# Float64 weights to float32: ScalarE's absolute value and two bounds in one VectorE operation

## The chip, the cores and the metric

The kernel runs on one core of a Trainium2 chip. The metric is the device time of one execution in microseconds (us). A core has five engines, each with an instruction stream of its own that it works through in order: TensorE (PE in the profile, its weight loads PEld), VectorE (DVE), ScalarE (ACT), GpSimd (POOL) and SyncE (SP, which here only issues DMAs).

## The reference, cut to what matters

```python
# attention part: x (8, 8, 512, 64), state (8, 8, 32, 64), float32
a  = softmax(x @ state.T / 8);  xread = a @ state
a2 = softmax(state @ x.T / 8);  sread = a2 @ x
x  = concatenate([xread, sread], axis=2) -> (4608 tokens, 512)
# first feed-forward part; w_gate, w_val (512, 1536), w_out (1536, 512): float64
g = x @ w_gate
x = (g * sigmoid(g) * (x @ w_val)) @ w_out
# second part: 8 experts of 576 tokens each, assigned greedily by the largest logits
logits = x @ gate;  out[mask] = relu(x[mask] @ w1[e]) @ w2[e]
```

The inputs are drawn as float32, but a division by a square root in numpy makes the three weights `w_gate`, `w_val` and `w_out` float64. They come to the chip as pairs of 32-bit words, and the kernel has to make float32 of them itself.

## The kernel before, in words

A matrix product in float32 is made of three: each operand is split into a rounded `hi` (ScalarE, a cast) and the rest `lo` (VectorE or GpSimd, a subtraction), and TensorE adds hi*hi, lo*hi and hi*lo.

There are three phases. The first, up to about 530 us of the profile, makes the hidden rows `ht` of the first feed-forward part; the second makes its output and the routing; the third runs the eight experts. All that follows is in the first phase, and there in its first three of four pairs of batches.

The work of the first phase is cut into 48 items: a pair of batches p (0 to 3) by a slice f of 128 hidden columns (0 to 11). In an item, `prepare` (L238) multiplies the states with the slice's weights (TensorE to `ps_x`), copies the result to `shi` (ScalarE, L258) and subtracts (VectorE, `slo`, L262); `hidden_part` (L264) then makes, for each of the two batches, 12 TensorE products of 512 columns into `pp` (L273), a Silu (ScalarE, `sg`, L277) and a product (VectorE, `ht`, L279). An item ends with its second `ht`, so there are 72 `ht` in the first 36 items.

Beside the items run: the attention of the 8 batches in 16 units (`attention`, L163: scores on TensorE, transposes and reductions on VectorE, two exponentials on ScalarE at L185 and L186, two products on GpSimd), and `narrow` (L69), which makes float32 of a half slice of 128 x 512 float64 numbers. It runs 36 times: 24 times for the gate and value weights, two for each slice f, and 12 times for the output weights (`weights_out`, L344). Slice f is needed by the item of pair 0 and slice f; until then the item waits.

Before the change `narrow` is a chain over the engines: DMA of 512 KB into `raw8`; VectorE bounds the high words (L81), shifts them (L84) and puts sign and exponent together (L85); ScalarE squares the bounded number (L88) and scales the low words (L89); GpSimd adds the two (L91); VectorE sets to zero what is too small (L93); ScalarE makes `hi` (L97) and GpSimd `lo` (L99).

The order on each engine is not written by hand in this part. The program is recorded as a loop over items with generators beside them (`beside`, L433): each `yield n` puts a generator off by n slots, five slots to an item, and the list `starts` (L419) says at which slot a narrowing begins. A scheduler with a timeline simulation then orders each engine's instructions. Only for the last pair of batches (items from `place[DIRECT, 0]` = 36) is TensorE's order fixed as recorded (`manual_schedule`). Silu and the exponentials belong to different ScalarE tables, and between them stands an `ACT_TABLE_LOAD`.

Of the kernel before, what the change touches and what calls it, by code (L numbers as in the profile page):

```python
# [9 lines left out]
F32 = mybir.dt.float32  # L10
F32R = mybir.dt.float32r
BF16 = mybir.dt.bfloat16
I32 = mybir.dt.int32
F16 = mybir.dt.float16
U8 = mybir.dt.uint8
U32 = mybir.dt.uint32
AF = mybir.ActivationFunctionType
OP = mybir.AluOpType
# [17 lines left out]
for _n, _w in (("before", 128), ("iota", 128), ("one", NT), ("rowhi", NT),  # L36
# [2 lines left out]
    CONSTS.append((_n, _o, _o + _w))  # L39
BEHIND = {"start": 36, "first": 26, "count": 19, "sum": 4, "totals": 17, "before": 14, "last": 18, "slots": 46,  # L40
          "places": 24}
LEAST = float(np.array([897 << 20], np.uint32).view(np.float32)[0])
LARGEST = float(np.array([(1150 << 20) | 0xFFFFF], np.uint32).view(np.float32)[0])


# [10 lines left out]
class Program:  # L56
# [12 lines left out]
    def narrow(self, src, hi=None, lo=None):  # L69

        nc, cv = self.nc, self.cv
        raw = cv.tile([128, 512, 2], I32, name="raw8", bufs=2)
        nc.sync.dma_start(raw.rearrange("p c t -> p (c t)"), src)
        yield 3
        c = cv.tile([128, 512], F32, name="cvc", bufs=3)  # L80
        nc.vector.tensor_scalar(c, raw[:, :, 1].bitcast(F32), -LARGEST, LARGEST, op0=OP.max, op1=OP.min)  # L81
        ci = c.bitcast(I32)
        t = cv.tile([128, 512], I32, name="cvt")
        nc.vector.tensor_scalar(t, ci, 3, 0x3FFFFFF8, op0=OP.logical_shift_left, op1=OP.bitwise_and)  # L84
        nc.vector.scalar_tensor_tensor(t, ci, -0x40000000, t, op0=OP.bitwise_and, op1=OP.bitwise_or)  # L85
        yield 1
        sq = cv.tile([128, 512], F32, name="cvs")
        nc.scalar.activation(sq, c, AF.Square)  # L88
        nc.scalar.activation(ci, raw[:, :, 0].bitcast(U32), AF.Copy, scale=2.0 ** -29)  # L89
        yield 1  # L90
        nc.gpsimd.tensor_tensor(t, t, ci, OP.add)  # L91
        yield 1
        nc.vector.scalar_tensor_tensor(c, sq, LEAST * LEAST, t.bitcast(F32), op0=OP.is_ge, op1=OP.mult)  # L93
        if hi is None:
            return c
        yield 1
        nc.scalar.copy(hi, c)  # L97
        yield 1
        nc.gpsimd.tensor_tensor(lo, c, hi.bitcast(F32), OP.subtract)  # L99
# [10 lines left out]

    def states(self, p):

        raw = self.cv.tile([128, 512], F32, name="cvs").rearrange("p (k c) -> p k c", k=4)
        self.nc.sync.dma_start(raw, self.a["sz"][p])
        yield 4
        self.state[p] = [self.sp.tile([128, 4, 128], F32R, name=n) for n in ("sh", "sl")]
        self.split(*self.state[p], raw, self.nc.gpsimd)
# [226 lines left out]
    def weights_out(self, f):  # L344

        nc = self.nc
        wo = yield from self.narrow(self.a["wo"][f // 2][:, 512 * (f % 2):512 * (f % 2) + 512].bitcast(I32))
        nc.sync.dma_start(self.wod[f // 2][:, f % 2], wo)
        yield 2
        pt = self.psl.tile([128, 4, 128], F32, name="ps_m")  # L350
        for k in range(4):
            nc.tensor.transpose(pt[:, k, :], wo[:, 128 * k:128 * k + 128], self.ident)
        yield 2
        both = self.cv.tile([128, 512], F32, name="cvs").rearrange("p (k c) -> p k c", k=4)
        nc.scalar.copy(both, pt)
        yield 2
        if f % 4 == 0:
            self.pf = self.psl.tile([128, 4, 128], F32, name="ps_l")
        for k in range(4):
            nc.tensor.matmul(self.pf[32 * k:32 * k + 32, f % 4, :], self.wg2[:, k, :], both[:, k, :],  # L360
                             start=True, stop=True)
        if f % 4 < 3:
            return
        yield 2
        fs = self.hp.tile([128, 512], F32, name="sg", bufs=2).rearrange("p (f c) -> p f c", f=4)
        nc.scalar.copy(fs, self.pf)
        yield 2
        pt = self.psl.tile([128, 4, 4, 32], F32, name="ps_m")
        for g in range(4):
            nc.tensor.transpose(pt[:, g].rearrange("p k e -> p (k e)"), fs[:, g, :], self.ident)  # L370
        yield 2
        nc.vector.tensor_reduce(self.wl[:, f - 3:f + 1, 0:E], pt[:, :, :, 0:E].rearrange("p g k e -> p g e k"),
                                AX.X, OP.add)

    def phase1(self, pools, first):

        tc, nc, a = self.tc, self.nc, self.a
        self.xp = first.enter_context(tc.tile_pool(name="xp", bufs=4))
        self.hp = first.enter_context(tc.tile_pool(name="hp", bufs=4))
        cv, lg, at, sp = ExitStack(), ExitStack(), ExitStack(), ExitStack()  # L380
# [17 lines left out]
        place = {item: n for n, item in enumerate(order)}  # L398
# [3 lines left out]
        def narrowed(f, m):  # L402
            if m == 0:
                w.append(self.wring.tile([128, 2, 1024], F32R, name="w"))
            q = slice(512 * m, 512 * m + 512)
            yield from self.narrow(a["wgv"][f][:, q].bitcast(I32), w[f][:, 0, q], w[f][:, 1, q])
            done[f] = m
# [10 lines left out]

        starts = []  # L419
        for f in range(1, NF):  # L420
            t = 5 * (place[0, f] - 1) - 8
            gap = 5 if f > LAG else 2
            starts += [(max(t - gap, 0), f, 0), (max(t, 0), f, 1)]

# [8 lines left out]
        def beside():  # L433

            f, rest = divmod(self.slot - self.OUTS, 5)
            if f == rest == 0:
                self.fold_start()
            if 0 <= f < NF and rest == 0:
                self.going.append([self.weights_out(f), 0, self.slot])
            while starts and starts[0][0] <= self.slot:  # L440
                self.going.append([narrowed(*starts.pop(0)[1:]), 0, self.slot])
            self.weights()
            for i, g in enumerate(list(self.going)):
                held = lambda lo, hi: sum(lo <= x[1] <= hi for x in self.going[1:] if x is not g)
                if g[2] > self.slot:
                    continue
                if i and (g[1] == 0 and held(1, 2) > 1 or g[1] == 1 and (held(2, 4) > 1 or held(2, 9) > 2)):
                    continue
                g[1] += 1
                d = next(g[0], None)  # L450
                if d is not None:
                    g[2] = self.slot + d
                elif i:
                    self.going.remove(g)
                else:
                    g[2] = 10000
            self.slot += 1

        def item(n, late):
# [11 lines left out]
            while n and not ready():  # L471
                beside()
            if ready():
                prep = self.prepare(*nxt, w[nxt[1]])
            next(prep, None)
            some(late, 1)
            beside()
            while self.atts.get(2 * p) != 1:
                beside()
# [43 lines left out]
        with tc.manual_schedule(engines={mybir.EngineType.PE}):  # L523
            for n in range(G, len(order)):
                p, f = order[n]
# [688 lines left out]
```

## Time and profile before

| | us |
|---|---|
| median of 3 runs | 1265.61 (1262.04 to 1266.66) |
| the profiled execution's own time | 1275.44 |
| its span, first to last instruction | 1273.5 |
| TensorE busy in the span | 1199.5 (94%) |
| VectorE busy | 822.3 (65%) |
| ScalarE busy | 543.7 (43%) |
| GpSimd busy | 284.0 (22%) |

The profiled execution took 0.8% longer than the median of the runs. The shares are averages over phases with different limits. In the page's slices of 31.8 us, VectorE is at 7 to 9 tenths in the first eight and TensorE at 5 to 8 tenths in the first five; from the sixth on TensorE is at 9.

### The profile page before, as it was taken

What the parts mean: (1) busy time and instruction counts of PE and PEld (TensorE: products, weight loads), DVE (VectorE), ACT (ScalarE), POOL (GpSimd) and SP (SyncE); (2) the same over time, 40 slices, a digit from 0 to 9 for tenths busy, and PEclk for the clock granted to TensorE, in tenths of its full rate; (3) what the DMA queues carried; (4) which work ended last, traced back from release to release, by engine and by line L of the source; (5) the groups of instructions that cost most, each with busy time, mean ns of one, the idle gap of its engine ahead of it and who ended that gap; (6) DMA issues with size and microseconds to landing.
All of it is one profiled execution on the core that took longest, in us unless ns stands there. A gap on an engine that the chain in (4) does not pass through costs nothing.

```text
span 1273.5 us, 21378 instructions
## 1 busy us (share of the span) xinstructions
PE 1199.5 (94%) x8127; PEld 980.6 (77%) x8127; DVE 822.3 (65%) x1730; ACT 543.7 (43%) x935; POOL 284.0 (22%) x247
## 2 busy tenths in 40 slices
PE   5888889999999999999999999979998999999998
PEld 2556668777786667877777777759897999999987
DVE  7999898768664443489989989735653444544310
ACT  4788877777753433411212122123432233343211
POOL 5665451313200000000000000032515135033031
PEclk9889999999999999999999999988998999999999
DMA  7555566345247877532333323257967365443110
GB/s 271 170 170 162 165 192 185 108 126 177 92 140 198 225 216 237 165 130 100 129 104 122 112 100 124 84 156 224 278 219 234 118 199 168 140 137 114 36 36 36
DMA packets 156309, 194.18 MB, mean 152 GB/s; under 512 B 14032, under 2 KB 119504, under 8 KB 156208
## 3 DMA queue, kind: packets, MB, share of 16 engines
q1 hardware_dynamic: 149904, 174.99, 43.9%
q0 software_dynamic: 6304, 17.83, 4.4%
q8 instruction: 64, 1.05, 0.3%
q14 instruction: 37, 0.30, 0.1%
HBM read 137.18 MB, written 55.51 MB: 151 GB/s over the span
## 4 chain that ended last, share of the span: by engine, by line
PE 69%; DVE 12%; issue 8%; ACT 6%; DMA 3%; POOL 1%; another core or an unknown queue 1%; ACTq 0%; SPq 0%; POOLq 0%; DVEq 0%
PE pp L898 18%; PE pp L273 17%; PE pu L1028 13%; PE pd L1063 7%; PE pd L1084 5%; PE ps_x L251 4%; ACT shi L258 2%; PE ps_s L312 1%; DVE cvt L85 1%; DVE slo L262 1%; PE ps_s L663 1%; DVE hlo L876 1%; DVE cvc L81 1%; DVE cvc L93 1%; ACT L277 1%
## 5 line engine op out<-in xcount | busy, mean ns | idle before, releaser
L898 PE MATMUL pp<-w,hhi 128*128 128x512 f32 x816 | 261.8, 398 | 0.0
L1028 PE MATMUL pu<-thi,w 128*128 128x256 f32 (+1 forms) x1024 | 213.6, 295 | 5.1 <-ACT thi L66 2.2
L898 PEld LDWEIGHTS pp<-w,hhi 128*128 128x128 f32 x816 | 151.5, 188 | 33.8 <-issue 2.5
L1028 PEld LDWEIGHTS pu<-thi,w 128*128 128x128 f32 x1024 | 171.5, 195 | 7.4 <-DVE ulo L1031 2.6
L273 PE MATMUL pp<-ahi,shi 128*128 128x512 f32 x384 | 159.3, 416 | 15.1 <-ACT sg L277 7.8
L898 PE MATMUL pp<-w,hlo 128*128 128x512 f32 x408 | 162.3, 398 | 1.2 <-DVE hlo L876 1.2
L262 DVE TENSOR_TENSOR slo<-ps_x,shi 64x512 fp32r<-64x512 f32 x192 | 131.9, 687 | 42.0 <-ACT shi L258 38.8
L273 PE MATMUL pp<-alo,shi 128*128 128x512 f32 x384 | 152.8, 399 | 0.0
L1028 PE MATMUL pu<-tlo,w 128*128 128x288 f32 (+1 forms) x512 | 150.9, 295 | 1.0 <-issue 0.8
L886 ACT CAST hhi<-hlo 128x768 fp32r<-128x768 f32 x68 | 53.4, 833 | 222.1 <-PE pp L898 219.4
L258 ACT CAST shi<-ps_x 64x512 fp32r<-64x512 f32 x192 | 111.5, 581 | 49.0 <-PE ps_x L251 41.8
L1031 DVE SCALAR_TENSOR_TENSOR ulo<-pu,uhi 128x256 fp32r<-128x256 f32 (+1 forms) x128 | 54.7, 437 | 114.2 <-ACT uhi L1030 106.5
L279 DVE TENSOR_TENSOR ht<-pp,sg 128x512 f32<-128x512 f32 (+1 forms) x108 | 71.3, 661 | 79.4 <-PE pp L273 41.3
L273 PE MATMUL pp<-ahi,slo 128*128 128x512 f32 x384 | 117.7, 394 | 0.1
L1030 ACT ACTIVATE uhi<-pu 128x256 fp32r<-128x256 f32 (+1 forms) x128 | 50.2, 398 | 151.1 <-PE pu L1028 128.0
L1063 PE MATMUL pd<-uhi,w 128*128 128x288 f32 x512 | 108.9, 297 | 6.1 <-issue 4.4
L273 PEld LDWEIGHTS pp<-ahi,shi 128*128 128x128 f32 x384 | 73.1, 191 | 46.5 <-ACT sg L277 12.1
L67 DVE TENSOR_TENSOR w<-raw,w 128x1024 fp32r<-128x1024 f32 x56 | 68.4, 1223 | 57.0 <-issue 34.2
L1028 PEld LDWEIGHTS pu<-tlo,w 128*128 128x128 f32 x512 | 99.7, 195 | 0.7 <-issue 0.4
L277 ACT ACTIVATE sg<-pp 128x512 f32<-128x512 f32 (+1 forms) x108 | 61.9, 575 | 79.6 <-PE pp L273 78.2
L1045 POOL DMA_INDIRECT out<-sw,idx x63 | 67.8, 1077 | 111.1 <-DVE sw L1069 93.3
L898 PEld LDWEIGHTS pp<-w,hlo 128*128 128x128 f32 x408 | 76.8, 188 | 18.1 <-DVE hlo L876 1.7
(242 smaller groups left out, 2178.8 us busy)
## 6 DMA issues: line engine op xcount, KB each, us to landing
raw<-w SPq DMA_DIRECT2D x64, 512.0 KB
hlo<-hd SPq DMA_DIRECT2D x34, 768.0 KB
hd<-ht SPq DMA_DIRECT2D x96, 256.0 KB
hraw<-hd SPq DMA_DIRECT2D x144, 128.0 KB
raw<-wgv SPq DMA_DIRECT2D x24, 512.0 KB
yd<-ys SPq DMA_DIRECT2D x32, 256.0 KB
xg<-row SPq DMA_DIRECT2D x28, 256.0 KB
row<-xg SPq DMA_DIRECT2D x112, 64.0 KB
```

What stands on the lines that cost most here:

```text
L67: lo_engine.tensor_tensor(lo, src, hi.bitcast(F32), OP.subtract)
L258: nc.scalar.copy(hi[r[z], b], banks[z][q])
L262: nc.vector.tensor_tensor(lo[r[z], b], banks[z][q], hi[r[z], b].bitcast(F32), OP.subtract)
L273: nc.tensor.matmul(pp, w(ws, k, m), xx[:, k, :], start=i == 0, stop=i == 3 * kt - 1)
L277: nc.scalar.activation(sg, pg, AF.Silu)
L279: nc.vector.tensor_tensor(ht, pv, sg, OP.mult)
L898: nc.tensor.matmul(py, x[:, f, :], wo[f // 2][:, f % 2, ws, :], start=i == 0, stop=i == 3 * NF - 1)
L1028: nc.tensor.matmul(pu, wf[:, ws, k, cs], x[xs][:, k, q], start=i == 0, stop=i == 11)
L1031: nc.vector.scalar_tensor_tensor(lo[:, f, q], pu, 0.0, hi[:, f, q].bitcast(F32), op0=OP.max, op1=OP.subtract)
L1045: st = self.nc.gpsimd.indirect_dma_start(out=out, in_=rows, in_offset=None, out_offset=bass.IndirectOffsetOnAxis(ap=at, axis=0))
L1063: nc.tensor.matmul(pd, wf[:, ws, f % 2, 128 * fb:128 * fb + 128], xs[:, f, T:], start=i == 0, stop=i == 23)
L1084: nc.tensor.matmul(pd, xs[:, f, 128 * t:128 * t + 128], wf[:, ws, f % 2, :], start=i == 0, stop=i == 23)
```

## The change

The magnitude is taken first, on ScalarE (`Abs`, read from the high words in place of VectorE's bounding). One VectorE operation then bounds it from below and above (`LEAST` becomes the least magnitude kept, instead of a threshold below which zero is written), two more shift and join it with the sign, which is read from the raw words. The Square on ScalarE and the last VectorE operation (L93) are gone, and the sum of GpSimd is the result. Buffers: three `raw8` instead of two, one `cvt` and one `cvs` instead of two. Slots: six instead of three between the DMA and the first operation, starts three slots earlier, and up to three narrowings waiting for their DMA instead of two.

```diff
-LEAST = float(np.array([897 << 20], np.uint32).view(np.float32)[0])
+LEAST = float(np.array([896 << 20], np.uint32).view(np.float32)[0])
...
-        raw = cv.tile([128, 512, 2], I32, name="raw8", bufs=2)
+        raw = cv.tile([128, 512, 2], I32, name="raw8", bufs=3)
         nc.sync.dma_start(raw.rearrange("p c t -> p (c t)"), src)
-        yield 3
+        yield 6
         c = cv.tile([128, 512], F32, name="cvc", bufs=3)
-        nc.vector.tensor_scalar(c, raw[:, :, 1].bitcast(F32), -LARGEST, LARGEST, op0=OP.max, op1=OP.min)
         ci = c.bitcast(I32)
-        t = cv.tile([128, 512], I32, name="cvt")
-        nc.vector.tensor_scalar(t, ci, 3, 0x3FFFFFF8, op0=OP.logical_shift_left, op1=OP.bitwise_and)
-        nc.vector.scalar_tensor_tensor(t, ci, -0x40000000, t, op0=OP.bitwise_and, op1=OP.bitwise_or)
+        nc.scalar.activation(c, raw[:, :, 1].bitcast(F32), AF.Abs)
         yield 1
-        sq = cv.tile([128, 512], F32, name="cvs")
-        nc.scalar.activation(sq, c, AF.Square)
-        nc.scalar.activation(ci, raw[:, :, 0].bitcast(U32), AF.Copy, scale=2.0 ** -29)
-        yield 1
-        nc.gpsimd.tensor_tensor(t, t, ci, OP.add)
-        yield 1
-        nc.vector.scalar_tensor_tensor(c, sq, LEAST * LEAST, t.bitcast(F32), op0=OP.is_ge, op1=OP.mult)
+        nc.vector.tensor_scalar(c, c, LEAST, LARGEST, op0=OP.max, op1=OP.min)
+        nc.vector.tensor_scalar(ci, ci, 3, 0x3FFFFFF8, op0=OP.logical_shift_left, op1=OP.bitwise_and)
+        nc.vector.scalar_tensor_tensor(ci, raw[:, :, 1], -0x40000000, ci, op0=OP.bitwise_and, op1=OP.bitwise_or)
+        t = cv.tile([128, 512], I32, name="cvt", bufs=1)
+        nc.scalar.activation(t, raw[:, :, 0].bitcast(U32), AF.Copy, scale=2.0 ** -29)
+        yield 2
+        nc.gpsimd.tensor_tensor(ci, ci, t, OP.add)
...
-            t = 5 * (place[0, f] - 1) - 8
+            t = 5 * (place[0, f] - 1) - 11
...
-                if i and (g[1] == 0 and held(1, 2) > 1 or g[1] == 1 and (held(2, 4) > 1 or held(2, 9) > 2)):
+                if i and (g[1] == 0 and held(1, 2) > 2 or g[1] == 1 and (held(2, 4) > 1 or held(2, 9) > 2)):
```

VectorE, near the start, the second half slice of the first weights (its transfer is `raw_126`), between operations of the first attention units (`sT`, `mx`, `m`). Line numbers after the change are lower by two from the middle of `narrow` on. Before:

```order
L81 TENSOR_SCALAR cvc<-raw_126 128x512
L176 STREAM_TRANSPOSE w<-ps_m 128x512
L181 TENSOR_REDUCE mx<-ps_m 128x1
L84 TENSOR_SCALAR cvt<-cvc 128x512
L188 TENSOR_SCALAR mx<-mx 128x1
L178 TENSOR_REDUCE m_148<-w 128x16
L182 TENSOR_SCALAR mx<-mx 128x1
L190 TENSOR_REDUCE m_141<-sT 128x16
L85 SCALAR_TENSOR_TENSOR cvt<-cvc,cvt 128x512
L189 RECIPROCAL mx<-mx 128x1
L93 SCALAR_TENSOR_TENSOR cvc<-cvs,cvt 128x512
```

And after, the same half slice:

```order
L85 TENSOR_SCALAR cvc<-cvc 128x512
L176 TENSOR_REDUCE m_148<-w 128x16
L188 TENSOR_REDUCE m_141<-sT 128x16
L180 TENSOR_SCALAR mx<-mx 128x1
L187 RECIPROCAL mx<-mx 128x1
L86 TENSOR_SCALAR cvc<-cvc 128x512
L189 TENSOR_SCALAR m_141<-m_141 128x16
L87 SCALAR_TENSOR_TENSOR cvc<-raw_126,cvc 128x512
```

Three operations stand where there were three and then, for the first half slice, L93; no operation of VectorE stands behind GpSimd's sum any more, and the first of the three now reads what ScalarE wrote.

ScalarE, in item 20 of 48, the same attention unit (`es`, `sT`) with its table loads. Before:

```order
L185 ACT_TABLE_LOAD
L185 ACTIVATE es,mx<-ps_s,mx 128x512
L186 ACTIVATE sT<-sT 128x512
L258 CAST shi<-ps_x 64x512 x2
L277 ACT_TABLE_LOAD
L277 ACTIVATE sg<-pp 128x512
```

After:

```order
L183 ACT_TABLE_LOAD
L183 ACTIVATE es,mx<-ps_s,mx 128x512
L275 ACT_TABLE_LOAD
L275 ACTIVATE sg<-pp 128x512
L184 ACT_TABLE_LOAD
L184 ACTIVATE sT<-sT 128x512
L353 COPY cvs<-ps_m 128x512
L83 ACTIVATE cvc<-raw_2654 128x512
L275 ACT_TABLE_LOAD
L275 ACTIVATE sg<-pp 128x512
```

A Silu has moved between the two exponentials of the unit, which makes four loads of two. In the whole program there are 28 loads before and 32 after; behind the 37th `sg` there are 12 and 16.

SyncE, the queue of the DMAs at the start. Before:

```order
L114 DMA cvs<-sz 128x512
L341 DMA wg_2257<-wg 128x4x8
L124 DMA xt<-xt 128x1024
L122 DMA st<-st 128x256
L78 DMA raw_299<-wgv 128x1024
```

After:

```order
L112 DMA cvs<-sz 128x512
L79 DMA raw_295<-wgv 128x1024
L339 DMA wg_2145<-wg 128x4x8
L122 DMA xt<-xt 128x1024
L120 DMA st<-st 128x256
```

The third transfer of weights stands ahead of the inputs of the second batch instead of behind them.

## Rows read from the trace of the kernel before

**Rows 1.** Windows up to 1st, 9th, 25th, 37th, 73rd `ht`: length, busy, clock, DMA.
```profile
core 0: us, PE busy (x) PEld busy (x) DVE busy (x) ACT busy (x) POOL busy (x), PEclk, DMA share, GB/s
0.00:44.80 44.80, 28.79 (x213) 15.71 (x214) 35.33 (x64) 26.30 (x55) 27.40 (x27) 0.85 0.71 240
44.80:110.30 65.50, 50.35 (x381) 34.98 (x380) 62.18 (x112) 56.01 (x100) 42.07 (x32) 0.95 0.53 169
110.30:183.50 73.20, 67.20 (x383) 50.29 (x382) 69.16 (x111) 58.39 (x101) 37.79 (x28) 1.00 0.58 170
183.50:227.50 44.00, 42.48 (x238) 34.09 (x238) 38.11 (x62) 29.94 (x53) 9.04 (x7) 1.00 0.59 185
227.50:383.00 155.50, 152.07 (x987) 118.93 (x986) 107.95 (x187) 110.84 (x192) 33.01 (x26) 1.00 0.42 128
```
**Rows 2.** Instruction groups of VectorE up to 383 us: busy us, mean ns | idle before.
```profile
L93 DVE SCALAR_TENSOR_TENSOR cvc<-cvs,cvt 128x512 f32<-128x512 f32 x36 | 33.1, 919 | 2.4 <-POOL cvt L91 2.2
L85 DVE SCALAR_TENSOR_TENSOR cvt<-cvc,cvt 128x512 int32<-128x512 int32 x36 | 30.6, 851 | 0.2
L81 DVE TENSOR_SCALAR cvc<-raw 128x512 f32<-128x512 f32 x36 | 22.0, 612 | 10.3 <-DMA raw<-wgv 8.7 <-PE ps_x L251 0.7 <-DMA raw<-wo 0.7
L84 DVE TENSOR_SCALAR cvt<-cvc 128x512 int32<-128x512 int32 x36 | 21.4, 594 | 0.4
L178 DVE TENSOR_REDUCE m<-sT 128x16 f32<-128x512 f32 x12 | 8.1, 673 | 0.0
```
**Rows 3.** Instruction groups of ScalarE up to 383 us.
```profile
L89 ACT ACTIVATE cvc<-raw 128x512 int32<-128x512 uint32 x36 | 24.3, 674 | 6.5 <-DVE cvt L85 4.7 <-issue 1.2 <-DVE mx L189 0.2
L88 ACT ACTIVATE cvs<-cvc 128x512 f32<-128x512 f32 x36 | 22.7, 630 | 15.6 <-DVE cvc L81 10.6 <-DVE cvc L93 4.0 <-POOL sl L67 0.8
L277 ACT ACT_TABLE_LOAD x14 | 18.0, 1283 | 0.2
```
**Rows 4.** Instructions of the tile `cvc`: duration ns min/median/max, first and last start.
```profile
L81 DVE TENSOR_SCALAR cvc<-raw x36: 384/427/1527, 7.5 to 312.8; 128x512 f32<-128x512 f32 x36
...
L84 DVE TENSOR_SCALAR cvt<-cvc x36: 362/427/1291, 7.9 to 313.8; 128x512 int32<-128x512 int32 x36
L85 DVE SCALAR_TENSOR_TENSOR cvt<-cvc,cvt x36: 628/683/1728, 9.5 to 315.4; 128x512 int32<-128x512 int32 x36
...
L93 DVE SCALAR_TENSOR_TENSOR cvc<-cvs,cvt x36: 626/688/1781, 15.9 to 331.3; 128x512 f32<-128x512 f32 x36
```
**Rows 5.** ScalarE's waits, 44.8 to 110.3 us: us in total, times, longest.
```profile
ACT cvs L88 <- DVE cvc L81: 2.2, 3, 1.7
...
ACT w L97 <- DVE cvc L93: 1.5, 2, 0.9
```
**Rows 6.** Timeline of ScalarE, 316 to 320 us: start, duration, instruction.
```profile
317.97 1.28 ACT L277 ACT_TABLE_LOAD   x1
319.27 0.60 ACT L277 ACTIVATE sg<-pp 128x512 f32<-128x512 f32 x1
```
**Rows 7.** Timeline of TensorE, same stretch and on, with idle time before.
```profile
319.92 0.50 PE L273 MATMUL pp<-ahi,shi 128*128 128x512 f32 x1 [0.35 <-ACT sg L277]
...
323.77 0.50 PE L273 MATMUL pp<-ahi,shi 128*128 128x512 f32 x1 [1.47 <-ACT sg L277]
```
**Rows 8.** VectorE waiting for a ScalarE cast, up to 420 us.
```profile
DVE slo L262 <- ACT shi L258: 23.8, 22, 3.2
```

More of the change, by code (lines that the diff above doesn't have):

```diff
@@ L111, in states @@
     def states(self, p):
-        raw = self.cv.tile([128, 512], F32, name="cvs").rearrange("p (k c) -> p k c", k=4)
+        raw = self.cv.tile([128, 512], F32, name="cvs", bufs=1).rearrange("p (k c) -> p k c", k=4)
         self.nc.sync.dma_start(raw, self.a["sz"][p])
@@ L353, in weights_out @@
         yield 2
-        both = self.cv.tile([128, 512], F32, name="cvs").rearrange("p (k c) -> p k c", k=4)
+        both = self.cv.tile([128, 512], F32, name="cvs", bufs=1).rearrange("p (k c) -> p k c", k=4)
         nc.scalar.copy(both, pt)
```

## The prediction

> **What bounds the kernel now.** I read the busy shares by slice first, then cut the first 383 us at the starts of the 1st, 9th, 25th, 37th and 73rd `ht`, because two `ht` make an item and the edited code works only there; last the groups of VectorE and ScalarE, and who waits for whom. The reader is to see in [rows 1] five stages, which I call A to E. In A (44.8 us), B (65.5) and C (73.2) VectorE is busy 35.3, 62.2 and 69.2 us. A begins with 7.5 us in which its first instruction (L81, first start in [rows 4]) waits for the weights, so nearly all the rest of these three stages is VectorE at work; TensorE is idle 16.0, 15.2 and 6.0 us. In D (44.0 us) and E (155.5) it turns round: TensorE is idle 1.5 and 3.4 us, VectorE 5.9 and 47.6. What the change saves on VectorE can therefore be cashed up to the 25th `ht` and hardly behind it. ScalarE is no bound now, but near it: 56.0 of 65.5 us in B.
>
> **The change part by part.**
>
> *The removed VectorE operation.* L93 runs 36 times at a mean of 919 ns, 33.1 us [rows 2]. Its median is 688 and its longest 1781 ns [rows 4]: part of the mean is stalls. If the stalls pass to its neighbours, 36 x 0.688 = 24.8 us go; if they go with it, 33.1. I use the mean and keep 24.8 as the other end.
>
> The trace shows the same spread for L85, 628 to 1728 ns [rows 4]. By the Trainium skill ("SBUF — State Buffer", "SBUF: two separate sides") VectorE operations with two SBUF inputs or in a two-port mode and GpSimd operations shut each other out for a whole instruction. By that rule, as GpSimd's work is not cut, the blocked time may move rather than vanish, and the saving over all 36 would be 24.8 instead of 33.1 us.
>
> *The three that stay.* The bounding is now read from a contiguous buffer, the joining (L87) from every second word of the raw data. L81 (every second word) and L84 (contiguous) have the same median of 427 ns [rows 4], so the stride costs nothing measurable there. I keep 612, 594 and 851 ns for the three; the new join is bounded by 0.68 (median of L85) and 0.92 us (mean of L93), which would be 2 us over the 28 by the 25th `ht`, either way.
>
> *ScalarE.* Square (630 ns) becomes Abs, read with a stride like L89 (674 ns) [rows 3]; I take 674, which is +0.04 each, 1.6 us over 36.
>
> *Moves.* Counted in the orders. By the 1st `ht` the four operations of a narrowing had been issued 6, 5, 5 and 4 times; after the change the three stand there 6 times each, and three large attention operations (0.673 us by L178) have moved behind. By the 9th: 15, 14, 14, 13 against 16, 15, 14, and two more attention operations have moved. By the 25th: 25, 25, 24, 24 against 28, 28, 28, and the attention is level again. So the new order runs up to four narrowings ahead.
>
> Stage A: VectorE -4 x 0.919 + 0.594 + 0.851 - 3 x 0.673 = -4.2 us. On SyncE the third transfer of weights now goes ahead of the second batch's inputs: 512 KB at the 240 GB/s of this stage [rows 1] is 2.2 us for those inputs, which I cost at nothing, since the first batch's attention covers it; without that cover it takes half of the gain. Behind GpSimd's sum there is one step less on the way to the first weights, which can make it better. I take -4.2 (between -7 and -2).
>
> Stage B: VectorE -9 x 0.919 + 0.612 - 0.851 - 2 x 0.673 = -9.8 us, to 52.4. ScalarE: two loads fewer (-2.6), 10 Abs for 9 Squares (+1.1), one more Copy (+0.7): -0.8, to 55.2 us. So ScalarE becomes the longer of the two. It was idle 9.5 us of B; of that it waited 2.2 us for L81 and 1.5 us for L93 [rows 5], both of which are gone. I take -0.8 - 3.7 = -4.5 us; the ends are -0.8 (ScalarE keeps all its waits) and -9.8 (it hinders nobody).
>
> Stage C: VectorE -11 x 0.919 + 2 x 0.612 + 2 x 0.594 + 4 x 0.851 + 5 x 0.673 = -0.9 us: what goes is filled with the narrowings run ahead and the attention coming back. ScalarE gets two more narrowings' first step (+1.8) and four more Copies (+2.7), to 62.9 of 73.2 us. I take 0, between -2 and +4.5.
>
> Stage D: VectorE loses over ten us more, but TensorE ends it. It can give back at most its own idle time, -1.5 us [rows 1].
>
> Stage E: four more table loads (16 for 12) of 1.283 us. In the trace a load between the exponentials and a Silu reaches TensorE: the Silu of [rows 6] starts as the load ends, and TensorE stands 0.35 and then 1.47 us in front of the unit whose exponentials were split [rows 7]. By the whole stage, 3.4 us idle for 12 loads is 0.29 each: +1.1 us for four. The ends are 0 and 2 split units at 1.82, +3.6. L93 is gone here too, but VectorE has 47.6 us to spare.
>
> A load takes 1.283 us, with 0.2 us of idle time before all 14 of L277 [rows 3], and the Silu starts 0.02 us behind one [rows 6]. The Trainium skill ("ScalarE: Activation LUTs", "What ACT_TABLE_LOAD costs") adds a drain of about 1.38 us to each: by that, as an estimate, four more would take ScalarE 10.6 instead of 5.1 us. This trace shows no such drain behind a load.
>
> *Sum.* -4.2 - 4.5 + 0 - 1.5 + 1.1 = -9.1 us on the profiled execution's 1275.4: 1266.3. The median of the runs stands at 1265.61 / 1275.44 = 0.9923 of it, so 1256.6 us. Nothing behind 383 us is changed but a few neighbours that trade places, so what is gained stays.
>
> **The rivals.**
>
> 1. *ScalarE hinders nobody* and the stages follow VectorE's sum: -4.2 - 9.8 - 0.9 - 1.5 = -16.4 us, 1249 us. For it: in B VectorE waits for almost nothing now (3.3 us idle). Against it: ScalarE's 55.2 us would have to fit into 55.7.
>
> 2. *ScalarE becomes the bound*: it keeps its waits in B (-0.8), D gives nothing, E has two more split units at 1.82 us: -4.2 - 0.8 + 3.6 = -1.4 us, 1264 us. For it: 86% busy in B and 80% in C already, and the chain now begins on it. Against it: a good part of its waits was for the removed operations.
>
> 3. *VectorE queues behind Abs*, slower. VectorE's first operation waited for a DMA before, which had long landed but for 8.7 us in all [rows 2]; now it waits for a place in ScalarE's order, and behind it stand `slo`, `ht` and the attention, which TensorE needs. Where VectorE waited for a cast of ScalarE, it was 23.8 us for 22 times, 1.08 each [rows 8]. By the 25th `ht` VectorE's sum is 14.9 us lower with 28 such first operations, so the case decides from 0.53 us per Abs on. If three of four wait 1.08, that is 22.7 - 14.9 + 1.1 = +8.9 us, 1274 us. Against it: only a small part of the `slo` waited at all, and the new order puts Abs well ahead of its VectorE operations.
>
> That the change does nothing in the program is excluded by the order: L93 is not in it.
>
> **How the numbers follow.** The forecast has a chance of 0.48, its own range 1251 to 1261; rival 1 0.17 (1244 to 1251), rival 2 0.23 (1259 to 1268), rival 3 0.12 (1266 to 1280). A change under 0.5% (6.3 us) can't be told from none, so faster means under 1259.3. From the forecast 0.43 and all of rival 1, and 0.02 of rival 2: 0.62. Slower than 1271.9 is most of rival 3: 0.09. The rest, 0.29, is the same. The range leaves out the far half of rival 3 and the far end of rival 1: 1244 to 1268.
>
> **What would show it.** Right: the 1st `ht` near 41 us, the 9th near 102, the 25th near 175, the 37th near 217, the 73rd near 374; VectorE's join and bounding at 0.6 to 0.9 us; ScalarE over 90% busy in B. Rival 1 has the 9th `ht` near 96; rival 2 the 9th near 105 and the 73rd near 382; rival 3 a line of VectorE's bounding waiting for ScalarE's Abs with over 15 us. The forecast would be wrong if E loses more than 4 us (table loads in front of TensorE), if the second batch's scores start late because of the moved transfer, or if Abs takes much longer than 0.67 us.

## The result, and the profile after

The changed kernel takes 1252.23 us (median of 4 runs, 1250.44 to 1255.98) against 1265.51 us of the kernel before (4 runs). The ratio is 0.9915 with a 95% interval of 0.9893 to 0.9938, faster by 0.85%. Two later runs on other chips gave 0.9906 (0.9887 to 0.9925) and 0.9911 (0.9891 to 0.9931).

The windows of the changed kernel, cut at the same `ht` as before (1st, 9th, 25th, 37th, 73rd), answer to [rows 1]:

```profile
0.00:39.30 39.30, 23.58 (x204) 12.82 (x208) 30.42 (x58) 26.55 (x53) 26.75 (x26) 0.96 0.81 279
39.30:95.70 56.40, 46.98 (x352) 33.20 (x340) 53.99 (x97) 49.58 (x90) 40.49 (x33) 0.91 0.64 197
95.70:171.10 75.40, 69.34 (x401) 52.10 (x399) 69.16 (x117) 67.61 (x118) 42.36 (x32) 1.00 0.68 204
171.10:217.20 46.10, 45.28 (x245) 33.88 (x246) 26.35 (x39) 24.84 (x45) 2.33 (x2) 1.00 0.32 95
217.20:375.50 158.30, 155.08 (x1016) 120.15 (x1012) 109.77 (x188) 117.31 (x198) 33.07 (x27) 1.00 0.44 130
```

By stage the change is -5.5, -9.1, +2.2, +2.1 and +2.8 us: 12.4 us won up to the 25th `ht`, 4.9 given back up to the 73rd, 7.5 kept. The spans of the two first profiles differ by far more, 22.3 us; the experiments show that most of the rest does not belong to the change.

VectorE's groups up to 380 us answer to [rows 2]. L93 has no successor; L85 is the bounding, L86 the shift, L87 the join:

```profile
L87 DVE SCALAR_TENSOR_TENSOR cvc<-raw,cvc 128x512 int32<-128x512 int32 x36 | 32.8, 911 | 0.3
L86 DVE TENSOR_SCALAR cvc<-cvc 128x512 int32<-128x512 int32 x36 | 24.3, 675 | 0.2
L85 DVE TENSOR_SCALAR cvc<-cvc 128x512 f32<-128x512 f32 x36 | 21.7, 605 | 2.8 <-ACT cvc L83 2.7
```

The four groups of before took 107.1 us, the three take 78.8: 28.3 us less, between the two ends named (24.8 and 33.1). The shift has grown from 594 to 675 ns and the join from 851 to 911: a part of the stalls of L93 went on to its neighbours. In the tile's durations (minimum, median, maximum) shortest and longest lie as in [rows 4], so the operations are not slower by themselves; what holds them is shown at the price of L93 below:

```profile
L85 DVE TENSOR_SCALAR cvc<-cvc x36: 357/428/1492, 9.5 to 303.6; 128x512 f32<-128x512 f32 x36
L86 DVE TENSOR_SCALAR cvc<-cvc x36: 357/476/1401, 10.5 to 304.3; 128x512 int32<-128x512 int32 x36
L87 DVE SCALAR_TENSOR_TENSOR cvc<-raw,cvc x36: 649/692/1662, 11.0 to 305.7; 128x512 int32<-128x512 int32 x36
```

ScalarE's groups, as in [rows 3]; L83 is the Abs:

```profile
L89 ACT ACTIVATE cvt<-raw 128x512 int32<-128x512 uint32 x36 | 24.4, 678 | 2.9 <-POOL cvc L91 2.8
L83 ACT ACTIVATE cvc<-raw 128x512 f32<-128x512 f32 x36 | 24.2, 672 | 11.2 <-DMA raw<-wgv 9.3 <-DMA wod<-cvc 1.5 <-POOL w L97 0.2
L275 ACT ACT_TABLE_LOAD x16 | 20.5, 1283 | 0.3
```

Abs took 672 ns, as estimated from the strided Copy (674). The wait for the weights' DMA, 8.7 us on VectorE before, is now on ScalarE with 9.3 us. What VectorE still waits for up to the 25th `ht` is little:

```profile
DVE sT L174 <- PE ps_s L169: 8.3, 1, 8.3
DVE m L188 <- ACT sT L184: 3.7, 1, 3.7
DVE mx L186 <- ACT es L183: 1.5, 1, 1.5
DVE ht L277 <- ACT sg L275: 1.1, 2, 0.7
DVE w L202 <- POOL w L191: 0.3, 1, 0.3
DVE cvc L85 <- ACT cvc L83: 0.2, 1, 0.2
```

The first line is the start; behind ScalarE VectorE stands 6.5 us in all, and behind Abs 0.2.

### The profile page after: what moved, and what is told of

It is laid out like the page before. It is cut to its first block, busy times and chain, and to the rows that moved or that the text cites. A ratio compares the mean times of both kernels' runs of the same rounds, so it can differ in the third digit from the quotient of the medians.

```text
span 1251.2 us, 21394 instructions
## 1 busy us (share of the span) xinstructions
PE 1191.4 (95%) x8127; PEld 973.5 (78%) x8127; DVE 799.0 (64%) x1694; ACT 548.8 (44%) x939; POOL 278.8 (22%) x247
## 4 chain that ended last, share of the span: by engine, by line
PE 68%; ACT 8%; DVE 8%; DMA 7%; issue 6%; SPq 1%; POOL 1%; POOLq 0%; ACTq 0%; DVEq 0%
PE pp L896 18%; PE pp L271 17%; PE pu L1026 12%; PE pd L1061 6%; PE pd L1082 5%; PE ps_x L249 4%; DMA raw<-w 3%; ACT shi L256 2%; PE ps_s L310 1%; ACT L275 1%; PE ps_s L661 1%; DVE hlo L874 1%; ACT sg L275 1%; SPq L1003 1%; DMA row<-yd,idx 1%
## 5 line engine op out<-in xcount | busy, mean ns | idle before, releaser
L1026 PE MATMUL pu<-thi,w 128*128 128x256 f32 (+1 forms) x1024 | 208.7, 290 | 0.4 <-ACT thi L66 0.4
L271 PE MATMUL pp<-ahi,shi 128*128 128x512 f32 x384 | 158.6, 414 | 13.8 <-ACT sg L275 6.7
L1026 PEld LDWEIGHTS pu<-thi,w 128*128 128x128 f32 x1024 | 168.1, 191 | 0.8 <-ACT thi L66 0.5
L271 PE MATMUL pp<-ahi,slo 128*128 128x512 f32 x384 | 120.5, 398 | 1.0 <-DVE slo L260 1.0
L1043 POOL DMA_INDIRECT out<-sw,idx x63 | 66.9, 1061 | 110.9 <-DVE sw L1067 93.1
```

The lines of the kernel that those rows point to most:

```text
L271: nc.tensor.matmul(pp, w(ws, k, m), xx[:, k, :], start=i == 0, stop=i == 3 * kt - 1)
L1026: nc.tensor.matmul(pu, wf[:, ws, k, cs], x[xs][:, k, q], start=i == 0, stop=i == 11)
L1043: st = self.nc.gpsimd.indirect_dma_start(out=out, in_=rows, in_offset=None, out_offset=bass.IndirectOffsetOnAxis(ap=at, axis=0))
```

## The experiments

All twelve in one table, then one by one. Up to the 25th `ht`, "busy" is VectorE's busy time and "idle" the rest. The times of different chips are not to be compared (chips differ by 6 us here for the same kernel), the ratios are. The 25th `ht` of one kernel depends less on the chip: 183.5 to 186.0 us in three traces of the kernel before, 170.1 to 171.3 in three of the changed one. e1 to e4 ran on one chip, e5 to e8 on a second, e9 to e12 on a third.

| run | median us | ratio to before (95%) | 25th `ht` | VectorE busy | idle | 73rd `ht` |
|---|---|---|---|---|---|---|
| before, first trace | 1265.51 | | 183.5 | 166.7 | 16.8 | 383.0 |
| after, first trace | 1252.23 | 0.9915 (0.9893 to 0.9938) | 171.1 | 153.6 | 17.5 | 375.5 |
| e1 before again | 1270.88 | 1.0008 (0.9987 to 1.0030) | 186.0 | 169.4 | 16.6 | 385.5 |
| e2 new arithmetic, old pace | 1269.04 | 1.0008 (0.9983 to 1.0034) | 180.7 | 154.2 | 26.5 | 383.0 |
| e3 old arithmetic, new pace | 1273.78 | 1.0040 (1.0024 to 1.0056) | 188.6 | 158.5 | 30.1 | 389.9 |
| e4 a fourth operation | 1280.08 | 1.0091 (1.0057 to 1.0124) | 188.2 | 173.9 | 14.3 | 392.4 |
| e5 after again | 1251.19 | 0.9906 (0.9887 to 0.9925) | 171.3 | 154.5 | 16.8 | 375.8 |
| e6 two raw buffers | 1253.69 | 0.9930 (0.9913 to 0.9946) | 177.7 | 152.2 | 25.5 | 376.4 |
| e7 short slots | 1259.89 | 0.9980 (0.9968 to 0.9992) | 176.6 | 159.0 | 17.6 | 380.5 |
| e8 exponentials together | 1258.95 | 0.9976 (0.9961 to 0.9991) | 179.1 | 160.5 | 18.6 | 381.9 |
| e9 before, same chip as e10 | 1262.84 | 1.0005 (0.9991 to 1.0019) | 186.0 | 168.9 | 17.1 | 385.5 |
| e10 after, same chip as e9 | 1250.97 | 0.9911 (0.9891 to 0.9931) | 170.1 | 152.7 | 17.4 | 374.5 |
| e11 no Abs | 1255.26 | 0.9943 (0.9923 to 0.9962) | 180.0 | 162.2 | 17.8 | 378.7 |
| e12 one slot more | 1254.78 | 0.9942 (0.9924 to 0.9960) | 172.8 | 155.7 | 17.1 | 376.2 |

**e1, e9 and e10: which part of the gain is the change's.** Unchanged kernels. Expected of e1, e9 and e10:

> The kernel before, unchanged, once more. Theory: in the first trace of before, 14.5 of the 22.3 us by which its span exceeds that of the changed kernel lie in the expert phase (intervals of 52.4, 55.6 and 50.3 us between experts where 48 is usual), which the change does not touch, so they are that execution's own. Then here the span is near 1263, the 73rd ht again near 383 us and the experts' phase shorter by about 8 us. Rival: the expert phase of before is always that long because of the order of its last instructions; then the phase takes about 416 us from the first pu to the end again, and ratio 1.000 with the earlier runs of before only if all are so.

> The kernel before once more, with the changed kernel behind it on the same chip, for the expert phase (first pu to the end): 413 and 417 us in two traces of before, 402 and 403 in two of the changed kernel, but no two of them from one chip. Theory C (the chip sets it): both phases within 3 us of each other, and the whole gain of 11 to 13 us less than 4 from outside the first 383 us. Theory K (the kernel sets it): before's at least 8 us longer here too.

> The changed kernel on the same chip as the run before it. 73rd ht at 375 to 377 us by either theory; expert phase within 3 us of that of before (theory C) or 8 us shorter (theory K). Ratio 0.989 to 0.993.

The stretch from the first `pu` of the experts to the end, in windows of the same columns as [rows 1]. Kernel before, first trace, e1 and e9:

```profile
857.00:1273.50 416.50, 399.16 (x2710) 378.30 (x2708) 176.93 (x296) 131.28 (x236) 123.49 (x116) 0.97 0.47 149
```

```profile
859.60:1273.00 413.40, 396.06 (x2710) 376.39 (x2708) 177.15 (x296) 131.76 (x236) 121.54 (x117) 0.97 0.47 150
```

```profile
858.80:1261.00 402.20, 392.58 (x2710) 374.00 (x2708) 177.18 (x295) 132.25 (x236) 122.62 (x116) 0.98 0.48 155
```

And e10, the changed kernel on e9's chip:

```profile
847.90:1249.00 401.10, 392.23 (x2710) 373.49 (x2708) 177.29 (x296) 132.24 (x236) 122.08 (x116) 0.99 0.48 155
```

The same instructions of the same kernel take 402 to 417 us; before and after on one chip are 1.1 us apart. The numbers of theory C came: the kernel does not set this phase. That the chip alone sets it is not shown, for the profiled execution of the kernel before took 9.8 us longer than the median of the other runs then. So e1's first theory was half right (the phase was not the change's) and half wrong (it did not shorten on e1's chip, and its span was 1273, not 1263). On e9's and e10's chip the spans are 12.0 us apart, and 11.0 of these are there at the 73rd `ht` (385.5 and 374.5, half a microsecond below what was expected). TensorE's granted clock does not make them: up to the 25th `ht` its mean is 0.97 in e9 and 0.94 in e10. Of the first two traces' 22.3 us, 14.2 were in the expert phase.

**e2 and e3: arithmetic or pace.** e2 has the new arithmetic with the pace of before:

```diff
-        raw = cv.tile([128, 512, 2], I32, name="raw8", bufs=3)
+        raw = cv.tile([128, 512, 2], I32, name="raw8", bufs=2)
-        yield 6
+        yield 3
-        yield 2            # ahead of GpSimd's sum
+        yield 1
-            t = 5 * (place[0, f] - 1) - 11
+            t = 5 * (place[0, f] - 1) - 8
-                ... held(1, 2) > 2 ...
+                ... held(1, 2) > 1 ...
```

e3 is the kernel before with the opposite edits and with one `cvt` and one `cvs` buffer, so that the third `raw8` has room.

> The new arithmetic (Abs, three VectorE operations) with the pacing of before: two raw8 buffers, slots 3 and 1 instead of 6 and 2, starts at 8 slots, two narrowings ahead instead of three. Theory that VectorE's load up to the 25th ht is what was saved: 1250 to 1257, the 25th ht at 175 us or earlier. Rival that the deeper prefetch and the new slots made the gain: 1261 to 1267, the 25th ht above 180 us.

> The arithmetic of before (four VectorE operations, Square) with the pacing and the buffers of the change (three raw8, one cvt, one cvs, slots 6, starts 11 earlier, three narrowings ahead). Theory of VectorE's load: no better than before, 1262 to 1270, 25th ht at 181 us or later. Rival of the pacing: 1250 to 1257, 25th ht near 172 us.

Neither has the gain: 1.0008 and 1.0040. By the 25th `ht` and the ratio e2 came out as its rival said, that the pace makes the gain, and e3 as the theory of the load said; so neither part makes it alone. In e3 VectorE is busy 158.5 us and idle 30.1, 13.8 of them behind ScalarE; what its single `cvt` and `cvs` do to the older chain was not separated from the pace. e2 up to the 25th `ht`:

```profile
0.00:180.70 180.70, 142.79 (x923) 98.51 (x924) 154.21 (x263) 139.44 (x252) 106.49 (x87) 0.93 0.61 196
```

VectorE is busy as little as in the changed kernel (154.2 and 153.6 us), but idle 26.5 instead of 17.5 us. Against e1 on the same chip it has 15.2 us less of VectorE's load, but its 25th `ht` is only 5.3 us earlier, and at the 73rd 2.5 us are left. VectorE's waits in e2:

```profile
DVE ht L277 <- ACT sg L275: 4.1, 5, 1.4
DVE slo L260 <- ACT shi L256: 3.1, 6, 1.3
...
DVE cvc L85 <- ACT cvc L83: 2.6, 4, 0.9
...
DVE m L188 <- ACT sT L184: 1.3, 1, 1.3
```

With the small ones it waits 11.7 us for ScalarE, where the changed kernel has 6.5, and mostly not for Abs but for what stands beside it on ScalarE. Abs itself waits 18.4 us for its data over the whole part, 9.3 in the changed kernel.

**e4: the removed load put back.** A fourth operation of L93's form that multiplies by one, ahead of GpSimd's sum, so that still nothing of VectorE stands behind the sum:

```diff
+        nc.vector.scalar_tensor_tensor(c, c, -3.0e38, c, op0=OP.is_ge, op1=OP.mult)
```

> The changed kernel with a fourth VectorE operation of the removed one's form (scalar_tensor_tensor, two SBUF inputs) put behind the third, which multiplies by one: the load on VectorE is back, the chain stays short (nothing of VectorE behind GpSimd's sum). Theory of the load: most of the gain is lost, 1259 to 1266, 25th ht 180 us or later. Rival that the shorter chain (no VectorE behind GpSimd) makes the gain: 1251 to 1256.

```profile
0.00:188.20 188.20, 147.12 (x934) 102.92 (x935) 173.94 (x286) 138.02 (x251) 107.08 (x85) 0.89 0.59 186
```

VectorE is busy 20.4 us more than in the changed kernel and the 25th `ht` is 17.1 us later; the whole gain is gone and 0.9% more. The rival falls that the gain comes from having nothing of VectorE behind GpSimd's sum: that is so here too. (Ahead of the sum the chain is one operation longer, which was not separated.) VectorE's load sets these stages, at 0.84 us of delay for each us of load that is added; taken away without the new pace, in e2 against e1, it gave back only 0.35. From the 25th to the 73rd `ht` e4 takes 204.2 us, as long as the changed kernel (204.4) and 4.7 us longer than e1: what the new order gives back there, e4 loses too.

**e5 to e7: which part of the pace.** e5 is the changed kernel on the chip of e6 to e8; e6 takes back the buffers and `held(1, 2) > 2` alone, e7 the slots and starts alone.

> The changed kernel, unchanged, on the chip on which the next three run. Theory that its expert phase (402 us from the first pu to the end in the first trace, 408 to 416 in the others) is its own, through the few instructions that stand in another order there: again 400 to 405 us, ratio 0.988 to 0.993. Rival that this was that execution's chance: 408 us or more, and a ratio of 0.993 to 0.997 carried by the first phase alone.

> The changed kernel with two raw8 buffers and two narrowings waiting for their DMA instead of three; its slots and starts stay. Theory A (new after the second run: the Abs stands in ScalarE's queue, so what pays is that its data are there; depth of the prefetch decides): Abs waits for DMA over 14 us in all, 25th ht at 178 us or later, ratio 0.997 to 1.003. Theory B (the longer slots decide, because they put the Abs later in the order): waits of Abs for DMA stay near 9 us, 25th ht near 172, ratio 0.988 to 0.994.

> The changed kernel with the slots and starts of before (3, 1, starts 8 earlier) and its three raw8 buffers and three narrowings ahead. Theory A (depth decides): as the changed kernel, 25th ht near 172, ratio 0.988 to 0.994. Theory B (slots decide): Abs waits for DMA over 14 us, 25th ht 178 or later, ratio 0.997 to 1.003.

e5's expert phase was 403.0 us, which seemed to say that it was the kernel's; e9 showed that it is not. e6 and then e7 up to the 25th `ht`:

```profile
0.00:177.70 177.70, 139.58 (x923) 98.38 (x924) 152.18 (x263) 146.12 (x260) 105.07 (x87) 0.93 0.62 199
```

```profile
0.00:176.60 176.60, 143.21 (x916) 97.38 (x916) 159.03 (x265) 143.50 (x258) 109.25 (x88) 0.94 0.64 209
```

In e6 VectorE is busy 152.2 us and idle 25.5; in e7 it is idle 17.6 but busy 159.0, 4.5 us more than in e5. So depth and slots do different things: without the third buffer VectorE waits, without the longer slots its instructions last longer.

By the whole time both runs fall into theory B's ranges: the slots are worth 0.7% (e7 against e5), the depth 0.2% (e6). By their mechanisms neither theory came out. The 25th `ht` is late in both, 177.7 and 176.6 us against 171.3 in e5, and Abs waits 12.4 us for its data in e6, neither over 14 nor near 9, and 8.6 in e7, where theory B wanted over 14. e6's whole time is nearer to the changed kernel than its 25th `ht`, because it gets back 4.6 us in the last stage: TensorE is not idle there at all, 3.2 us in the changed kernel, and there are 10 table loads instead of 16.

**e8: fewer table loads.**

```diff
-        nc.scalar.activation(es, ps, AF.Exp, bias=mx[:, 1:2], scale=SCALE, accum_out=mx[:, 2:3])
-        nc.scalar.activation(sT, sT, AF.Exp, scale=SCALE)
+        first = nc.scalar.activation(sT, sT, AF.Exp, scale=SCALE)
+        with self.tc.issue_after(first.ins):
+            nc.scalar.activation(es, ps, AF.Exp, bias=mx[:, 1:2], scale=SCALE, accum_out=mx[:, 2:3])
```

> The changed kernel with the two exponentials of an attention unit in a fixed order, the state's first and the other issued behind it, so that no Silu comes between: 26 table loads instead of 32. Forecast's theory that each load costs TensorE 0.3 us behind the 37th ht: the stretch from the 37th to the 73rd ht 156 us or less (158.3 now), ratio 0.001 to 0.003 better than the changed kernel. Rival that table loads are covered, or that es waiting for the other exponential costs as much: 158 us or more, no better or worse.

The last stage, with 10 loads in it:

```profile
226.40:381.90 155.50, 154.63 (x1022) 120.49 (x1019) 111.68 (x188) 109.95 (x192) 32.68 (x27) 1.00 0.46 136
```

It takes 155.5 us against 158.3, and TensorE is idle 0.9 us against 3.2, so the number expected of this stage came. A price for each load does not follow: TensorE's idle time there is 0.0 to 0.9 us with 10 loads (e6, e8, e11), but 3.4 with 12 (before) and 3.2 with 16 (after). And the kernel as a whole is slower than the changed one, since up to the 25th `ht` VectorE is busy 160.5 instead of 154.5 us (e5). The expected gain in the total was missed.

**e11: no Abs.** VectorE's first operation reads the raw words itself.

```diff
-        nc.scalar.activation(c, raw[:, :, 1].bitcast(F32), AF.Abs)
-        nc.vector.tensor_scalar(c, c, LEAST, LARGEST, op0=OP.max, op1=OP.min)
+        nc.vector.tensor_scalar(c, raw[:, :, 1].bitcast(F32), LEAST, LARGEST, op0=OP.max, op1=OP.min)
```

> The changed kernel without the Abs: VectorE's first operation reads the raw high words itself, so a negative weight becomes the least magnitude with its sign (this part of the computation is changed). ScalarE has 36 x 0.67 = 24 us less, VectorE the same, and the wait for the DMA is VectorE's again. Theory of the forecast, that ScalarE was near its bound in the 2nd stage and hindered: the 9th ht at 93 us or earlier, the 25th at 167 or earlier, ratio 0.984 to 0.989. Rival that VectorE alone binds these stages and ScalarE hinders nobody: 25th ht 169 to 175, ratio 0.989 to 0.994. Second rival, that the DMA wait belongs better on ScalarE than in front of VectorE's queue: 25th ht over 175, ratio over 0.995.

ScalarE is busy 132.9 instead of 143.7 us up to the 25th `ht`, and that `ht` comes 9 to 10 us later. So ScalarE's load was no bound there, against the forecast's theory. The second rival's number came, but not its mechanism: VectorE waits for the weights' DMA once, 7.7 us at the start. It is busy longer, 162.2 us. The bounding has become slower, with the Abs gone and the instructions around it in another order:

```profile
L84 DVE TENSOR_SCALAR cvc<-raw x36: 388/569/1520, 7.7 to 306.3; 128x512 f32<-128x512 f32 x36
```

Median 569 instead of 428 ns, shortest and longest as ever. Of these 36, 22 began while a GpSimd operation ran and were held by it, as is shown at the price of L93 below; in e10 it was 16. Whether the missing Abs or the new order does that was not tested by itself.

**e12: one slot more.** `yield 7` for `yield 6`, starts at 12 instead of 11 slots.

> The changed kernel with seven instead of six slots between the DMA and the Abs and starts one slot earlier: the same instructions in a slightly other order. If the pacing acts through the DMA's arrival alone, which is covered at six slots already (3.6 us of waits behind the first): ratio as the changed kernel, 0.989 to 0.993. If any shift of the order moves the time by as much as the pacing did (7 us): over 0.995 or under 0.987.

0.9942, between the two expectations: a third of the gain is lost by a shift that changes no instruction. Abs waits for its DMA only at the start (6.4 us). What is lost is VectorE's time, busy 3.0 us longer up to the 25th `ht` than in e10: 5.9 more in the third stage, 2.9 less in the second.

## Why the prediction was right, step by step

The time, 1252.23 us for a forecast of 1256.6, lies in the range and on the forecast side: 9.1 us were forecast on the profiled execution, and 11.3 to 13.3 us came by the medians, 11 of them in the first 383 us on one chip. The mechanism, VectorE's load up to the 25th `ht`, is shown by e4, and by the column "idle": with the third buffer and the new arithmetic it stays at 17 to 19 us (14 in e4) while the 25th `ht` moves with the busy time. But single terms were off: B gave 4.6 us more than forecast, D and E together 5.3 us less. That these two errors offset each other was luck.

- *Stage A*, forecast -4.2: measured -5.5 (-6.3 between e9 and e10). Right. The moved transfer cost nothing that shows: the waits of TensorE and of its weight loads for the inputs of the scores come to 10.0 us (6.3, 2.7 and 1.0), where they had come to 11.0.
- *Stage B*, forecast -4.5: measured -9.1 (-10.0). This is the step that failed. I let ScalarE become the bound with 55.2 us; it was busy 49.6 (88% of the stage, not over 90): the attention work that moved behind took its exponentials and copies along, which I had left out, and more of ScalarE's instructions than counted ran only in C (67.6 us instead of the 62.9 worked out there). VectorE's own sum, -9.8, was rival 1's number and the right one, and the 9th `ht` at 95.7 us is rival 1's sign. e11, with still less on ScalarE, shows no gain from it.
- *Stage C*, forecast 0: +2.2 (+0.4). Inside its bounds.
- *Stage D*, forecast -1.5, measured +2.1: wrong in sign. TensorE is as full as said (idle 0.8 us), but it has more to do. One attention unit's work, 5 units' scores in A before and 4 after, now stands here:

```profile
L206 PE MATMUL ps_s<-xn,es 128*32 128x64 f32 x32 | 2.2, 230 | 0.0
L169 PE MATMUL ps_s<-xt,st 128*64 128x512 f32 x4 | 2.1, 618 | 0.0
```

- *Stage E*, forecast +1.1, measured +2.8: the four loads are there (16 against 12), but TensorE's idle time is 3.2 us after 3.4. The stage has grown by TensorE work that came behind, 3.0 us, and not by the loads. What a load costs here is not settled (e8).

Over the five stages TensorE's busy time is the same (340.9 and 340.3 us), so the gain is its idle time, 42.1 to 35.2. I had read that for each stage apart, as if the work in it stayed.

- *The price of L93*: 28.3 us of 33.1 by the sum of the groups; of L93's 8.3 us above its median, 4.8 went to its neighbours. The Trainium skill's rule ("SBUF — State Buffer", "SBUF: two separate sides"), by which such a VectorE operation and a GpSimd operation shut each other out for a whole instruction, gives 24.8 if all of the blocked time moves. On the shutting out the traces agree, but part of the time vanished. L93's longest, with the GpSimd operation beside it (start, duration):

```profile
181.15 1.48 POOL L99 TENSOR_TENSOR w<-cvc,w 128x512 fp32r<-128x512 f32 x1
181.39 1.78 DVE L93 SCALAR_TENSOR_TENSOR cvc<-cvs,cvt 128x512 f32<-128x512 f32 x1
```

So it is in all fourteen traces: every bounding or shift of `narrow` over 435 ns and every other of its VectorE operations over 700 ns, 668 in all, began while a GpSimd operation ran (43 of 144 in the kernel before, 51 of 108 in the changed one). The bounding and the shift ended 0.28 to 0.29 us behind that one's end, the others 0.54 to 0.56. None of the rest lasted over 433 or 695 ns.

The time so lost (above the medians of those not held) up to the 25th `ht` is 27.0 us before and 21.3 after, 29.3 and 20.4 in e9 and e10: about half of what VectorE saved there. The order decides how often the two engines meet. The 84 operations of 28 narrowings up to the 25th `ht` take 63.5 us in the changed kernel and 70.9, 72.9, 71.7 and 66.9 in e7, e8, e11 and e12; of this 21.3, then 28.6, 30.7, 29.6 and 24.3 are lost to GpSimd, and what remains is 42.1 to 42.6 in all five.

- *Rival 3*, VectorE behind Abs: it waits 0.2 us for it up to the 25th `ht`. Its mechanism is seen in e2 and e6, in a weaker form: there VectorE waits 11.7 and 12.8 us for ScalarE, but for `sg`, `shi` and the exponentials more than for Abs.
- *The pace*: I had priced the third buffer and the slots at nothing apart from the moves they cause. e2 shows that without them nothing is won that could be told from none. The forecast held because I counted on the order as built, in which their effect is contained.

What stays open: e7, e8, e11 and e12 lose their time by operations that meet GpSimd, and e6 by waits; how much of that is due to their edit and how much to the order that the scheduler happens to build is not separated. No version beat the changed kernel.

## What to carry to other kernels

Cut the profile where the bound changes, and cash a saved operation only in the stages that its engine ends; but follow the work over the cuts, since what a new order takes out of one stage comes back in a later one. A shorter chain that begins on a busy in-order engine has to have its data in time: the same arithmetic was worth 0.9% with one more buffer and longer slots, and nothing that could be told from none without. When VectorE operations differ in length for the same shape, look what GpSimd runs beside them: about half of what VectorE saved here was time of being held, and the next order can bring it back. Before a phase that the change does not touch is credited to it, run both kernels on one chip.

## What the runs showed of the hardware that had not been expected

The expert phase of one unchanged program took 402.2, 413.4 and 416.5 us in three executions, with TensorE idle 9.6, 17.3 and 17.3 us. TensorE itself was busy longer for the same 2710 products, 392.6, 396.1 and 399.2 us, and its granted clock stood at the lower of its two levels (1.2 GHz) for 13.1, 20.9 and 24.1 us of the phase. On the chip of e1 to e4 it took 408 to 415 us in four programs, on the two others 401 to 405 in eight; why is not settled.

VectorE's bounding of 128 x 512 numbers had a mean of 591 ns in e10 and 811 in e11, with nearly the same shortest and longest: the mean follows how many of them met a GpSimd operation. `slo`, with one operand in PSUM, was not lengthened so: in the first trace of the kernel before, 56 of 152 up to the 73rd `ht` began during a GpSimd operation, the longest of them with 697 ns, of the others 695.
